# Four buffers for gathered token rows in the experts, and transpositions six steps ahead instead of seven

## The chip, the cores and the metric

The kernel runs on one core of a Trainium2 chip. A core has TensorE (matrix products, writing to PSUM), VectorE, ScalarE and GpSimd (elementwise work), SyncE (which here issues most transfers) and 16 DMA engines between HBM and the on-chip memory SBUF. Each engine works through its own queue in order. The metric is the device time of one execution, in microseconds.

## The reference, cut to what matters

Three networks in a row: attention with a threshold, a mixture of eight experts with one expert for each token, and a dense network with h - tanh(h) in the middle.

```python
# 4 sequences, 8 heads, 576 positions, 64 columns
scores = 1/sqrt(64) * q @ k.T
scores = where(scores >= max(scores) - tau, scores, -1e9)
x = softmax(scores) @ v                      # -> 2304 tokens x 512
logits = x @ w_gate                          # 512 x 8
expert_idx = argmax(logits, axis=1)
gate_w = softmax(logits)[expert_idx]
for e in range(8):
    xe = x[expert_idx == e]
    out[expert_idx == e] = gate_w * (maximum(xe @ w1[e], 0) @ w2[e])   # 512 -> 1024 -> 512
h = out @ w_in                               # 512 -> 2048
return (h - tanh(h)) @ w_out                 # 2048 -> 512
```

## The kernel before, in words

The kernel writes every instruction out by hand, in program order; a small table of numbers (`TB`) sets in which *step* of the expert and dense stages each job stands. The order on each engine is the program order, and the framework adds the waits.

**Attention** fills the first 350 us. Its results go to a table of token rows in HBM (`rows`, 512 columns in FP32), and the gate's logits L gather in SBUF (128 partitions x 8 experts x 18 tokens).

**Routing** (`route`) finds each token's expert and its place there, almost wholly on VectorE: a maximum over the experts, a comparison, a second maximum that breaks ties, the one-hot O, two matmuls for prefix counts, a prefix sum (`rst` restarts it at each expert), and some twenty small operations. It ends with 18 comparisons B (L656; the profile names the line of the helper, L597), which with R (L654, GpSimd) are the operands of 18 matmuls; their result `idx` lists, in columns of 128, the tokens of each expert. Small tiles of the routing live in three places: constants in a pool `c` for the whole program, `keep` and `free` in the expert stage's pool, whose room the attention stage has used before.

**Experts.** The experts are sorted by size, and each has a fixed capacity: 256, 544, 416, 384, 336, 320, 288 and 272 tokens. There are nine *passes* (the second expert has two, of 256 and 288). A pass p begins at step g = 8p and has eight steps. In each step TensorE computes the hidden product of 128 hidden units for the pass's tokens (`h_exp`, L1040, 12 matmuls: the FP32 operands are split in a high and a low half, three products each), then come the step's jobs, then the product with w2 for the step before last (`y_exp`, L1095, 12 matmuls into four PSUM tiles). ScalarE and VectorE make the high and low half of the ReLU (`relu`, L1075 and L1076) at the start of a step. `y` tiles of finished passes are copied by ScalarE (`yo`, L1098) and stored.

The jobs of steps: weight loads (`wload`) and splits (`wsplit`, L1008 on ScalarE and L1010 on VectorE or GpSimd), conversions of the dense network's weights (`conv`, L1155 to L1166), the late part of the routing (`route_late`), and for each chunk m of up to 128 tokens of a pass three jobs: `gather_exp` (L1057, an indirect DMA that GpSimd issues, into a buffer `xr`, in step g - 10 + m), `trans` (L1017, four transpositions by TensorE into the one PSUM tile `t`, in step g - 7 + m), and `evac` (L1027 on ScalarE and L1031 on VectorE, the split into high and low halves `xa`, right behind it). Pass 0 gathers ahead of the steps, transposes in steps -7 and -6, and uses two other PSUM tiles. Between steps -6 and -5, at -5.5, stand `offsets` and `starts` (L673, L680 and small operations of the helpers L570 and L573): 15 VectorE operations that compute where each pass's result goes. Steps below 0 hold jobs alone. The buffers `xr` are three; in the dense stage `x_load` uses them too.

**The dense network** takes the last 450 us, on six blocks of 384 tokens, 16 steps each.

Of the kernel before, what the change touches and what calls it, by code (L numbers as in the profile page):

```python
# [11 lines left out]
F32 = mybir.dt.float32  # L12
F32R = mybir.dt.float32r
F16 = mybir.dt.float16
# [4 lines left out]
ALU = mybir.AluOpType  # L19
# [4 lines left out]
B, H, S, D = 4, 8, 576, 64  # L24
NT, DM = B * S, H * D
# [403 lines left out]
E, F1, F2 = 8, 1024, 2048  # L429
# [6 lines left out]
NTL = 18  # L436
# [30 lines left out]
class Moe:  # L467
# [24 lines left out]
    def consts(self):  # L492
        nc, c, one = self.nc, self.cp.tile, self.attn.one.tile
        z = one([1, DM], F32, name="zrow")
        nc.gpsimd.memset(z, 0.0)
        nc.sync.dma_start(out=self.xtok[ZR:ZR + 1], in_=z)
        self.wg = c([128, 4, E], F32, name="wg")
        nc.sync.dma_start(out=self.wg, in_=self.wgd.rearrange("(k p) e -> p k e", p=128))
        self.i8 = self.iota("i8", E)
        self.r8 = self.iota("r8", E, -1, E)  # L500
        self.j8 = self.iota("j8", E, 1, -1)
        nc.gpsimd.memset(self.j8[:, 0:1], float(E - 1))
        self.i128 = self.iota("i128", 128)
        self.i128h = c([128, 128], F16, name="i128h")
        nc.vector.tensor_copy(self.i128h, self.i128)
        self.ina8 = self.iota("ina8", NMAIN, 128)
        rt = c([128, (E + 2) * NTL], F32, name="rt")
        self.m, self.tm = rt[:, 0:NTL], rt[:, NTL:2 * NTL]
        self.eq = rt[:, 2 * NTL:].rearrange("p (e t) -> p e t", e=E)
        self.ina = self.iota("ina", NMAIN)  # L510
        self.k18 = self.iota("k18", NTL, 128)
        ones = one([128, 128], F32, name="ones")
        nc.gpsimd.memset(ones, 1.0)
        tri = one([128, 128], F32, name="tri")
        nc.gpsimd.affine_select(out=tri, in_=ones, compare_op=ALU.is_gt, fill=0.0, base=0,
                                pattern=[[1, 128]], channel_multiplier=-1)
        self.onesh = c([128, 128], F16, name="onesh")
        self.trih = c([128, 128], F16, name="trih")
        nc.vector.tensor_copy(self.onesh, ones)
        nc.vector.tensor_copy(self.trih, tri)  # L520
        self.O = c([128, E, NTL + 1], F16, name="O")
        nc.gpsimd.memset(self.O, 0.0)

        self.rst = c([128, E, NTL + 1], F32, name="rst")
        nc.gpsimd.memset(self.rst, 1.0)
        nc.gpsimd.memset(self.rst[:, :, 0:1], 0.0)

        self.rc = c([128, 2, E], F32, name="rc")
        for r in range(E):
            b = 128 * CB[r]  # L530
            for i, x in enumerate((b, CAPS[r])):
                nc.gpsimd.memset(self.rc[:, i, r:r + 1], float(x))

        ti = one([128, NTL], I32, name="tok_i")
        for P in range(NP):
            b0, t0 = 2 * P * S + P - ZR, 9 * P
            for i in range(2):
                q = slice(64 * i, 64 * i + 64)
                for o, n, b in ((0, 4, b0 + i), (4, 1, b0 + (S if i else 8)), (5, 4, b0 + S + 1 + i)):
                    nc.gpsimd.iota(ti[q, t0 + o:t0 + o + n], pattern=[[2, n]], base=b, channel_multiplier=9)  # L540
        self.tok = c([128, NTL], F32, name="tok")
        nc.vector.tensor_copy(self.tok, ti)
# [29 lines left out]
    def red(self, o, a, op=ALU.add):  # L572
        self.nc.vector.tensor_reduce(out=o, in_=a, axis=AX.X, op=op)  # L573
# [12 lines left out]
    def route(self, K, T, psum):  # L586


        nc, cp = self.nc, self.cp
# [6 lines left out]
        k_out = lambda x: x.unsqueeze(2).to_broadcast([128, E, E])  # L596
        ts = lambda o, x, s1, s2, op0, op1=None: V.tensor_scalar(out=o, in0=x, scalar1=s1, scalar2=s2, op0=op0, **({"op1": op1} if op1 else {}))  # L597

        m, eq, tm = self.m, self.eq, self.tm
        red(m, te(L), ALU.max)  # L600
        tt(eq, L, bt(m), ALU.is_equal)
        tt(eq, eq, be(self.r8), ALU.mult)
# [16 lines left out]
        loc, lo, h1, ov = K([128, NTL], I32), T([128, NTL]), T([128, NTL]), K([128, NTL])  # L619
# [3 lines left out]
        B, R = T([128, NTL, 128], F16), T([128, NTL, NMAIN], F16)  # L623
# [29 lines left out]
        tt(A, self.ina8.unsqueeze(1).to_broadcast([128, NTL, NMAIN]), h1.unsqueeze(2).to_broadcast([128, NTL, NMAIN]), ALU.is_equal)  # L653
        nc.gpsimd.tensor_tensor(out=R, in0=A, in1=self.tok.unsqueeze(2).to_broadcast([128, NTL, NMAIN]), op=ALU.mult)  # L654
        for t in range(NTL):
            ts(B[:, t], self.i128h, lo[:, t:t + 1], None, ALU.is_equal)  # L656

        self.idx = cp.tile([128, NMAIN], I32, name="idx")
        self.table(B, R, psum("h", [128, NMAIN]), self.idx)
# [239 lines left out]
NW = MB * 128  # L899
# [19 lines left out]
class Mlp(Moe):  # L919
# [57 lines left out]
    def at(self, i, f, *a):  # L977
        self.sched.setdefault(i, []).append((f, a))
# [27 lines left out]
    def wsplit(self, r, i, j):  # L1006
        h, l, raw = self.W.pop((r, i, j, "raw"))
        self.nc.scalar.copy(h, raw)  # L1008
        pool = j if r < E else self.TB["eng"][2 * i + j] == "P"
        (self.nc.gpsimd if pool else self.nc.vector).tensor_tensor(out=l, in0=raw, in1=h.bitcast(F32), op=ALU.subtract)  # L1010
# [41 lines left out]

    def gather_exp(self, p, m, n):
        r, c0, _ = PASS[p]
        t = self.sp.tile([128, DM], F32, tag="xr", name="xr", bufs=3)
        c = CB[r] + c0 // 128 + m
        self.nc.gpsimd.indirect_dma_start(out=t[0:n], out_offset=None, in_=self.xtok, in_offset=bass.IndirectOffsetOnAxis(  # L1057
            ap=self.idx.bitcast(U32)[0:n, c:c + 1], axis=0))
        self.xr["e", p, m] = t
# [114 lines left out]
    def x_load(self, k):  # L1174
        nc = self.nc
        c = slice(NW * k, NW * k + NW)
        self.gb = self.sp.tile([128, DM], F32, tag="xr", name="xr", bufs=3)[:, 0:NW]
        nc.sync.dma_start(out=self.gb, in_=self.gscr.rearrange("(o a) b -> o (a b)", o=1)[:, c].to_broadcast([128, NW]))
        self.xw = []
        for d in range(4):  # L1180
            n, tg, nb = (NW, "yu"[d % 2], 2) if k == 0 else (DM, "xr", 3) if d < 2 else (1024, "raw", 4)
            w = self.sp.tile([128, n], F32, tag=tg, name="xw", bufs=nb)[:, 0:NW]
            nc.sync.dma_start(out=w, in_=self.yT[d][:, c])
            self.xw.append(w)
        t = self.sp.tile([128, max(6 * NMAX, 8 * NW)], F32R, tag="lxb" if k % 2 else "lxa", name="xk")
        t = t[:, 0:8 * NW].rearrange("p (a k n) -> p a k n", a=2, k=4)
        self.xs["l", k] = [(0, t[:, 0], t[:, 1])]
# [70 lines left out]
    def early2(self):  # L1258

        for i, j in FIRST:  # L1260
# [1 line left out]

    TB = {"wl": (4, 5), "ws": (2, 3), "ga": 10, "tr": 7, "ev": 7,
          "last": ((-3, -2), (-1, 1), (-2, 0), (0, 2), (-1, 2), (0, 3), (1, 2), (4, 6), (-60, -55), (-53, -50), (-7,
                  -1), (-6, -4), (5, 10), (9, 11), (11, 12), (12, 14)), "x0": (12, 9, 7), "x": (14, 13, 8),
          "conv": (0, 1, 3, 5, 7, 10, 11, 13, 15, 16, 18, 20, 21, 23, 25, 28, 29, 32, 33, 35, 37, 38, 40, 42, 44, 46,
# [2 lines left out]
    def plan(self, K):  # L1271
        at = self.at
        for p, (r, c0, n) in enumerate(PASS):
            g = 8 * p
            at(g - 8, self.x_exp, p)
            for m in range(-(-n // 128)):
                w = min(128, n - 128 * m)
                if p:
                    at(max(g - self.TB["ga"], -8) + m, self.gather_exp, p, m, w)
                at(g - self.TB["tr"] + m, self.trans, ("e", p, m), w)  # L1280
                at(g - self.TB["ev"] + m, self.evac, ("e", p, m), 128 * m, w)
        B = self.TB
        at(-5.5, self.offsets)
# [75 lines left out]
```

## Time and profile before

| what | value |
|---|---|
| median of 3 runs | 1076.59 us (1075.49 to 1080.34) |
| the profiled execution | 1076.63 us |
| its span, first to last instruction | 1074.5 us |
| granted TensorE clock, mean over the span | 0.944 of 2.4 GHz |
| routing, logits complete to idx | 350.0 to 361.8 us |
| expert stage, first hidden product | 369.95 us |

The profile gives each engine's busy time, what an engine waited for, and the granted clock of TensorE in any stretch. Times within the execution count from the first instruction. A wait that the profile calls "issue" has no releaser that it can name. A row's bracket tells how long the engine was idle before it and what ended that.

### The profile page before, as it was taken

What the parts mean: (1) busy time and instruction counts of PE and PEld (TensorE: products, weight loads), DVE (VectorE), ACT (ScalarE), POOL (GpSimd) and SP (SyncE); (2) the same over time, 40 slices, a digit from 0 to 9 for tenths busy, and PEclk for the clock granted to TensorE, in tenths of its full rate; (3) what the DMA queues carried; (4) which work ended last, traced back from release to release, by engine and by line L of the source; (5) the groups of instructions that cost most, each with busy time, mean ns of one, the idle gap of its engine ahead of it and who ended that gap; (6) DMA issues with size and microseconds to landing.
All of it is one profiled execution on the core that took longest, in us unless ns stands there. A gap on an engine that the chain in (4) does not pass through costs nothing.

```text
span 1074.5 us, 20770 instructions
## 1 busy us (share of the span) xinstructions
PE 957.3 (89%) x7342; PEld 876.6 (82%) x7342; DVE 895.3 (83%) x1635; ACT 671.5 (62%) x1262; POOL 730.7 (68%) x645
## 2 busy tenths in 40 slices
PE   4688897887787488999999988999999999999997
PEld 3576786776677387989999988888999999998986
DVE  5899888888884698977798876998989889888894
ACT  5797887986974154444455557666665666656662
POOL 3897887886874364455656567787867768677763
PEclk9698888898988599999999999999999999999999
DMA  6798999998989485877787976220101101000000
GB/s 160 145 213 165 211 205 152 225 202 163 175 155 169 149 292 199 278 227 247 258 290 252 295 247 177 76 76 20 40 8 38 30 20 40 8 31 1 20 11 30
DMA packets 247368, 153.16 MB, mean 143 GB/s; under 512 B 179642, under 2 KB 222028, under 8 KB 247261
## 3 DMA queue, kind: packets, MB, share of 16 engines
q1 hardware_dynamic: 243501, 141.02, 53.2%
q0 software_dynamic: 3312, 10.49, 2.8%
q8 instruction: 59, 0.97, 0.4%
q14 instruction: 48, 0.39, 0.1%
q10 hardware_dynamic: 448, 0.30, 0.1%
HBM read 85.08 MB, written 23.60 MB: 101 GB/s over the span
## 4 chain that ended last, share of the span: by engine, by line
PE 50%; DVE 9%; issue 3%; DMA 2%; ACT 1%; POOL 0%; another core or an unknown queue 0%; POOLq 0%; DVEq 0%; SPq 0%; ACTq 0%
PE h L1040 25%; PE y L1123 15%; PE y L1095 9%; DVE w L1236 2%; DVE w L1237 2%; PE t L1017 1%; DVE w L1234 1%; DMA xr<-rows,idx 1%; DVE cv L1157 1%; DVE tm L1235 1%; DVE w L1238 1%; DMA raw<-in_moe_w_dram 1%; DVE w L1010 1%; DMA raw<-wscr 0%; DVE cm L1159 0%
## 5 line engine op out<-in xcount | busy, mean ns | idle before, releaser
L265 POOL TENSOR_TENSOR e<-em,e 128x1024 f16<-128x1024 f32 (+1 forms) x98 | 158.1, 1613 | 55.0 <-ACT e L261 23.5
L1233 POOL TENSOR_SCALAR tm<-u 128x384 uint8<-128x384 f32 x88 | 129.7, 1474 | 51.4 <-ACT u L1229 50.8
L1040 PE MATMUL h<-xa,w 128*128 128x256 f32 (+6 forms) x864 | 140.5, 313 | 7.6 <-DVE hbuf L1076 6.8
L1095 PE MATMUL y<-hbuf,w 128*128 128x256 f32 (+6 forms) x864 | 139.5, 310 | 0.6 <-ACT yo L1098 0.6
L1040 PEld LDWEIGHTS h<-xa,w 128*128 128x128 f32 x864 | 130.5, 194 | 9.9 <-DVE hbuf L1076 8.1
L240 ACT ACTIVATE e<-sps,n 128x576 f32<-128x576 f32 x144 | 110.6, 768 | 34.8 <-DVE n L234 33.7
L1010 POOL TENSOR_TENSOR w<-raw,w 128x1024 fp32r<-128x1024 f32 x36 | 91.8, 2551 | 56.0 <-ACT w L1008 28.8
L1095 PEld LDWEIGHTS y<-hbuf,w 128*128 128x128 f32 x864 | 127.5, 191 | 1.3 <-ACT yo L1098 0.8
L1236 DVE SCALAR_TENSOR_TENSOR w<-y,w 128x384 f32<-128x384 f32 x96 | 123.3, 1284 | 0.0
L1229 ACT ACTIVATE u<-h 128x384 f32<-128x384 f32 x96 | 47.1, 491 | 117.3 <-PE h L1040 116.4
L253 DVE SCALAR_TENSOR_TENSOR em<-sps,n,e 128x576 f32<-128x576 f32 x144 | 116.6, 810 | 4.0 <-ACT e L240 2.4
L234 DVE TENSOR_REDUCE n<-sps 128x1 f32<-128x576 f32 x144 | 107.1, 744 | 12.3 <-PE sps L226 11.8
L1250 POOL TENSOR_TENSOR gl<-w,gh 128x384 fp32r<-128x384 f32 x83 | 85.7, 1032 | 38.0 <-ACT gh L1249 38.0
L1040 PE MATMUL h<-xk,w 128*128 128x384 f32 x576 | 109.6, 338 | 0.7 <-DVE w L1010 0.5
L297 PE MATMUL ops<-vh,et 128*128 128x64 f16 (+1 forms) x2240 | 97.4, 201 | 13.0 <-DVE x L303 12.1
L1040 PEld LDWEIGHTS h<-xk,w 128*128 128x128 f32 x576 | 102.1, 188 | 5.6 <-DVE w L1010 1.3
L297 PEld LDWEIGHTS <-et 128*128 128x128 f16 (+1 forms) x2240 | 83.6, 107 | 25.3 <-issue 21.1
L261 ACT CAST e<-em 128x576 f16<-128x576 f32 x144 | 99.9, 695 | 1.2 <-DVE em L253 1.2
L1075 ACT ACTIVATE hbuf<-h 128x256 fp32r<-128x256 f32 (+6 forms) x72 | 31.2, 433 | 108.3 <-PE h L1040 108.2
L226 PE MATMUL sps<-ka,qa 128*128 128x288 f32 x320 | 87.7, 367 | 9.4 <-DVE em L253 5.7
L1008 ACT CAST w<-raw 128x1024 fp32r<-128x1024 f32 x72 | 75.6, 1051 | 21.4 <-DVE free L597 11.6
L1123 PE MATMUL y<-w,gh 128*128 128x512 f32 x258 | 81.1, 395 | 3.2 <-POOL w L1010 1.5
(228 smaller groups left out, 2296.8 us busy)
## 6 DMA issues: line engine op xcount, KB each, us to landing
raw<-in_moe_w_dram SPq DMA_DIRECT2D x64, 512.0 KB, 5.2
cv<-in_moe_w_in_dram SPq DMA_DIRECT2D x16, 512.0 KB, 5.0
cv<-in_moe_w_out_dram SPq DMA_DIRECT2D x16, 512.0 KB, 5.4
wscr<-cm SPq DMA_DIRECT2D x32, 256.0 KB, 3.2
raw<-wscr SPq DMA_DIRECT2D x16, 512.0 KB, 3.8
xw<-yT SPq DMA_DIRECT2D x24, 192.0 KB, 2.7
vv<-in_v_dram SPq DMA_DIRECT2D x8, 512.0 KB, 5.1
raw<-in_q_dram SPq DMA_DIRECT2D x6, 576.0 KB, 7.7
```

Source lines behind the costliest of these rows:

```text
L234: nc.vector.tensor_reduce(out=n[:, 0:1], in_=ps[:, :, 0:288], axis=AX.XY, op=ALU.max, negate=True)
L240: nc.scalar.activation(out=e, in_=ps[:, :, 0:288], func=AF.Exp, bias=n[:, 0:1])
L253: nc.vector.scalar_tensor_tensor(out=self.em[u, g][:, i].rearrange("p (a b) -> p a b", a=2), in0=ps[:, :, 0:288], scalar=n[:, 1:2], in1=e, ...
L261: self.nc.scalar.copy(self.e16[u, g][:, i, 0:S], self.em[u, g][:, i])
L265: eng.tensor_tensor(out=e16[:, r, S + 64:], in0=em[:, r, 0:512], in1=e16[:, r, 0:512], op=ALU.subtract)
L297: nc.tensor.matmul(o[q], lhsT=et[:, base + c, q], rhs=vh[:, a, j, c if c < 5 else c - 5, :], start=(n == 0), stop=(n == len(terms) - 1))
L1010: (self.nc.gpsimd if pool else self.nc.vector).tensor_tensor(out=l, in0=raw, in1=h.bitcast(F32), op=ALU.subtract)
L1040: self.nc.tensor.matmul(out, lhsT=a, rhs=b, start=(i == 0), stop=(i == len(parts) - 1))
L1095: nc.tensor.matmul(self.ys[d], lhsT=a[:, f % 2, s], rhs=b, start=(f == 0 and i == 0), stop=(f == 7 and i == 2))
L1123: nc.tensor.matmul(self.ys[m], lhsT=a[:, s], rhs=b[:, f % 2], start=(f == 0 and i == 0), stop=(f == 15 and i == 2))
L1233: nc.gpsimd.tensor_scalar(out=mk, in0=u, scalar1=RCUT * RCUT, scalar2=None, op0=ALU.is_gt)
L1236: V.scalar_tensor_tensor(out=w, in0=y, scalar=b, in1=w, op0=ALU.add, op1=ALU.mult)
```

## The change

Room is made in SBUF and spent on a fourth buffer `xr`; with it, `trans` and `evac` stand in step g - 6 + m instead of g - 7 + m, while the gathers keep their steps. The room comes from constants: the gate weights move to a pool of the attention stage, the FP16 copy of the row 0..127 goes (B then reads the FP32 row), the tiles for the comparison and the second maximum move to the scratch `free`, and `rst` is FP16.

```diff
-        self.wg = c([128, 4, E], F32, name="wg")
+        self.wg = one([128, 4, E], F32, name="wg")
...
-        self.i128h = c([128, 128], F16, name="i128h")
-        nc.vector.tensor_copy(self.i128h, self.i128)
...
-        rt = c([128, (E + 2) * NTL], F32, name="rt")
-        self.m, self.tm = rt[:, 0:NTL], rt[:, NTL:2 * NTL]
-        self.eq = rt[:, 2 * NTL:].rearrange("p (e t) -> p e t", e=E)
+        self.m = c([128, NTL], F32, name="m")
...
-        self.rst = c([128, E, NTL + 1], F32, name="rst")
+        self.rst = c([128, E, NTL + 1], F16, name="rst")
...
-        m, eq, tm = self.m, self.eq, self.tm
+        m, eq, tm = self.m, T([128, E, NTL]), T([128, NTL])
...
-            ts(B[:, t], self.i128h, lo[:, t:t + 1], None, ALU.is_equal)
+            ts(B[:, t], self.i128, lo[:, t:t + 1], None, ALU.is_equal)
...
-        t = self.sp.tile([128, DM], F32, tag="xr", name="xr", bufs=3)
+        t = self.sp.tile([128, DM], F32, tag="xr", name="xr", bufs=4)
...
-    TB = {"wl": (4, 5), "ws": (2, 3), "ga": 10, "tr": 7, "ev": 7,
+    TB = {"wl": (4, 5), "ws": (2, 3), "ga": 10, "tr": 6, "ev": 6,
```

The same `bufs` stands in `x_load`. The order of instructions on GpSimd and on SyncE is the same in both kernels. On VectorE, at the start of the expert stage, this stood before (`xa` is the split of a chunk; `keep` and `poff` are the operations of `offsets` and `starts`; `hbuf` is the low half of the ReLU):

```order
L1031 TENSOR_TENSOR xa<-y_6252,xa 128x4x128
L1031 TENSOR_TENSOR xa<-y_6260,xa 128x4x128
L570 TENSOR_TENSOR keep<-keep 128x64
L573 TENSOR_REDUCE keep<-keep 128x8
L673 SCALAR_TENSOR_TENSOR keep<-rst,keep 128x8
L570 TENSOR_TENSOR keep<-keep 128x8
L570 TENSOR_TENSOR keep<-keep 128x64
L573 TENSOR_REDUCE keep<-keep 128x8
L680 TENSOR_SCALAR poff<-keep 128x1 x9
L1076 SCALAR_TENSOR_TENSOR hbuf<-h,hbuf 128x256 x2
L1031 TENSOR_TENSOR xa<-t,xa 128x4x128
```

and this stands there now, at the same place of VectorE's queue:

```order
L1027 TENSOR_TENSOR xa<-y_6251,xa 128x4x128
L566 TENSOR_TENSOR keep<-keep 128x64
L569 TENSOR_REDUCE keep<-keep 128x8
L669 SCALAR_TENSOR_TENSOR keep<-rst,keep 128x8
L566 TENSOR_TENSOR keep<-keep 128x8
L566 TENSOR_TENSOR keep<-keep 128x64
L569 TENSOR_REDUCE keep<-keep 128x8
L676 TENSOR_SCALAR poff<-keep 128x1 x9
L1027 TENSOR_TENSOR xa<-y_6273,xa 128x4x128
L1072 SCALAR_TENSOR_TENSOR hbuf<-h,hbuf 128x256 x3
L1027 TENSOR_TENSOR xa<-t,xa 128x4x128
```

The split of pass 0's second chunk has moved behind the 15 operations of `offsets` and `starts`, and the split of pass 1's first chunk behind the ReLU of step 2.

Further on in VectorE's queue, in steps 9 to 11, where pass 2's first two chunks are split (`cv` and `cm` are a conversion, `w` is a weight split), this stood before:

```order
L1159 TENSOR_SCALAR cm<-cv 128x512
L1076 SCALAR_TENSOR_TENSOR hbuf<-h,hbuf 128x256
L1031 TENSOR_TENSOR xa<-t,xa 128x3x128
L1031 TENSOR_TENSOR xa<-t,xa 128x128
L1164 SCALAR_TENSOR_TENSOR cm<-cv,cm 128x512
L1076 SCALAR_TENSOR_TENSOR hbuf<-h,hbuf 128x256
L1031 TENSOR_TENSOR xa<-t,xa 128x3x128
L1031 TENSOR_TENSOR xa<-t,xa 128x128
L1010 TENSOR_TENSOR w_6625<-raw,w_6624 128x1024
```

and this stands there now:

```order
L1155 TENSOR_SCALAR cm<-cv 128x512
L1072 SCALAR_TENSOR_TENSOR hbuf<-h,hbuf 128x256
L1160 SCALAR_TENSOR_TENSOR cm<-cv,cm 128x512
L1072 SCALAR_TENSOR_TENSOR hbuf<-h,hbuf 128x256
L1027 TENSOR_TENSOR xa<-t,xa 128x3x128
L1027 TENSOR_TENSOR xa<-t,xa 128x128
L1006 TENSOR_TENSOR w_6623<-raw,w_6622 128x1024
```

Each chunk's split stands one ReLU half later. On TensorE the four transpositions of a chunk stand one hidden product and one y product later in the same way, from pass 1 on.

## Rows read from the trace of the kernel before

**Rows 1.** The page's engine totals: busy us, share of the span, instructions.

```profile
PE 957.3 (89%) x7342; PEld 876.6 (82%) x7342; DVE 895.3 (83%) x1635; ACT 671.5 (62%) x1262; POOL 730.7 (68%) x645
```

**Rows 2.** Stretches: length, busy PE, PEld, DVE, ACT, POOL (instructions), clock, DMA share, GB/s.

```profile
366.00:400.00 34.00, 30.56 (x220) 28.92 (x220) 25.48 (x42) 14.95 (x24) 19.55 (x12) 0.87 0.78 258
400.00:420.00 20.00, 13.92 (x105) 13.57 (x105) 16.36 (x29) 9.43 (x21) 10.92 (x7) 0.91 0.63 207
...
500.00:540.00 40.00, 40.00 (x239) 39.85 (x238) 32.40 (x42) 19.68 (x36) 22.28 (x14) 1.00 0.80 260
```

**Rows 3.** Waits of TensorE, 366 to 620 us: us in total, times, longest.

```profile
PE h L1040 <- DVE hbuf L1076: 4.6, 3, 2.5
PE t L1017 <- issue: 4.5, 1, 4.5
PE t L1017 <- DMA xr<-rows,idx: 1.6, 1, 1.6
```

**Rows 4.** Timeline, end of attention and routing: start us, us, instruction, idle before.

```profile
348.24 0.62 SPq L316 DMA_DIRECT2D rows<-x  x1
...
350.70 0.31 DVE L570 TENSOR_TENSOR rt<-L,rt 128x144 f32<-128x144 f32 x1
...
352.59 0.47 DVE L626 TENSOR_TENSOR_SCAN keep<-rst,t 128x152 f32<-128x152 f32 x1 [0.46 <-PE t L608]
```

**Rows 5.** The line of that store (L316), 347.5 to 349 us.

```profile
DMA to landing us min/median/max: 2.7/2.7/2.7
```

**Rows 6.** VectorE's B (ns min/median/max), and a copy (us, mean ns).

```profile
L597 DVE TENSOR_SCALAR free<-i128h,free x18: 241/243/962, 357.6 to 361.1; 128x128 f16<-128x128 f16 x18
...
L505 DVE CAST i128h<-i 128x128 f16<-128x128 f32 x1 | 0.2, 227 | 0.0
```

**Rows 7.** Timeline of VectorE and of TensorE's weight loads, start of the experts.

```profile
369.25 1.38 DVE L1031 TENSOR_TENSOR xa<-y,xa 128x512 fp32r<-128x512 f32 x2 [4.72 <-ACT xa L1027]
370.54 0.25 DVE L570 TENSOR_TENSOR keep<-keep 128x64 f32<-128x64 f32 x1
...
371.89 0.63 DVE L680 TENSOR_SCALAR poff<-keep 128x1 int32<-128x1 f32 x9
373.90 0.42 DVE L1076 SCALAR_TENSOR_TENSOR hbuf<-h,hbuf 128x256 fp32r<-128x256 f32 x1 [1.39 <-ACT hbuf L1075]
...
370.68 4.66 PEld L1040 LDWEIGHTS h<-xa,w 128*128 128x128 f32 x23 [0.44 <-DVE xa L1031]
```

**Rows 8.** Timelines of VectorE and of TensorE, 378 to 393 us.

```profile
378.81 0.69 DVE L1031 TENSOR_TENSOR xa<-t,xa 128x512 fp32r<-128x512 f32 x1 [0.47 <-ACT xa L1027]
...
392.11 0.41 DVE L1076 SCALAR_TENSOR_TENSOR hbuf<-h,hbuf 128x256 fp32r<-128x256 f32 x1
...
392.57 1.70 PE L1040 MATMUL h<-xa,w 128*128 128x256 f32 x12 [1.47 <-DVE hbuf L1076]
```

**Rows 9.** Timeline of TensorE, steps 9 to 11.

```profile
401.65 0.63 PE L1017 MATMUL t<-ident,xr 128*128 128x128 f32 x4 [1.62 <-DMA xr<-rows,idx]
...
409.62 1.09 PE L1017 MATMUL t<-ident,xr 128*128 128x128 f32 x4 [4.46 <-issue]
410.36 2.60 PE L1095 MATMUL y<-hbuf,w 128*128 128x256 f32 x12
412.80 1.58 PE L1040 MATMUL h<-xa,w 128*128 128x256 f32 x12
```

**Rows 10.** Timeline of the other engines in the same steps.

```profile
404.19 2.52 DVE L570 TENSOR_TENSOR keep<-keep 128x18 int32<-128x18 f32 x1
404.30 2.37 POOL L1010 TENSOR_TENSOR w<-raw,w 128x1024 fp32r<-128x1024 f32 x1
...
408.72 1.19 ACT L1098 COPY yo<-y 128x256 f32<-128x256 f32 x4
408.77 0.74 DVE L1031 TENSOR_TENSOR xa<-t,xa 128x384 fp32r<-128x384 f32 x2
```

**Rows 11.** A stretch behind the longer wait; columns as in rows 2.

```profile
411.00:412.00 1.00, 1.00 (x7) 1.00 (x7) 0.58 (x2) 1.00 (x3) 0.55 (x1) 0.50 0.36 125
```

More of the change, by code (lines that the diff above doesn't have):

```diff
@@ L1176, in x_load @@
         c = slice(NW * k, NW * k + NW)
-        self.gb = self.sp.tile([128, DM], F32, tag="xr", name="xr", bufs=3)[:, 0:NW]
+        self.gb = self.sp.tile([128, DM], F32, tag="xr", name="xr", bufs=4)[:, 0:NW]
         nc.sync.dma_start(out=self.gb, in_=self.gscr.rearrange("(o a) b -> o (a b)", o=1)[:, c].to_broadcast([128, NW]))
@@ L1180, in x_load @@
         for d in range(4):
-            n, tg, nb = (NW, "yu"[d % 2], 2) if k == 0 else (DM, "xr", 3) if d < 2 else (1024, "raw", 4)
+            n, tg, nb = (NW, "yu"[d % 2], 2) if k == 0 else (DM, "xr", 4) if d < 2 else (1024, "raw", 4)
             w = self.sp.tile([128, n], F32, tag=tg, name="xw", bufs=nb)[:, 0:NW]
```

## The prediction

> **What bounds the kernel now.** I first read the engine totals of the page, to see which engine could set the span: TensorE is busy for 957.3 of 1074.5 us [rows 1], so only about 117 us of the span are open to any change that does not take work off TensorE. Then I read the busy times by stretch from the end of the routing on [rows 2]. The reader should see two different stages there. Between 366 and 400 us TensorE is busy for 30.56 of 34.00 us, between 400 and 420 us for 13.92 of 20.00; between 500 and 540 us it is busy for all 40.00 us. The table of waits for 366 to 620 us says who caused the gaps [rows 3]: the change speaks of two of them, a transposition of gathered rows that waits 1.6 us for its gather and one that waits 4.5 us for something that the profile cannot name ("issue"); 4.6 us more are waits of the hidden product for the ReLU's low half on VectorE. From 500 us on TensorE has no gap to close [rows 2], so the reachable gain lies ahead of that, and it cannot be much more than 1.6 + 4.5 + 4.6 = 10.7 us of waits plus the slow clock behind them.
>
> **Part by part: the routing.** The five first routing operations wrote tiles of their own; now the comparison and the maximum behind it write to the stage's scratch tile, whose room the attention stage used. So the wait for that stage's last stores, which stood at the prefix sum, stands two operations after the logits are complete. Before, the comparison began at 350.70 us and the prefix sum at 352.59 us [rows 4]. The last store is issued at 348.24 us [rows 4] and lands 2.7 us later [rows 5], at 350.94. So the comparison waits 350.94 - 350.70 = 0.24 us, and behind it in VectorE's queue is the whole routing, on which the gathers depend: +0.2 us on the path. Bounds: nothing, if the other engines' waits cover it, and 352.59 - 350.70 = 1.9 us, since the same wait was over by the prefix sum.
>
> The 18 one-hot rows B read a 128-column row of FP16 before and one of FP32 now. One took 243 ns in the median, one 962 ns, beside the GpSimd operation on R [rows 6]. No row shows the FP32 form. The nearest one is a copy of the same 128 columns from FP32 to FP16, 227 ns [rows 6], no slower than the old form; so the lower end is 0. The upper end is the FP32 tensor-tensor operation of 144 columns, 0.31 us [rows 4], 66 ns more, 18 x 66 = 1.2 us. I take 0.3 us, near the copy, all on the path, since the table's last matmul needs the last B. The prefix sum's data0 in FP16, the removed copy of i128 in the attention stage, and the gate weights in another pool I cost at nothing: the sum already mixes types with its PSUM operand, the copy is one of 227 ns [rows 6] in a stage with other work on VectorE, and the load of the gate weights is the same transfer.
> The Trainium skill ("VectorE: DVE Perf Modes", section "The perf-mode tier table") gives a tensor-scalar operation four elements a cycle for 16-bit operands and two for FP32. By that each B costs 32 cycles at 0.96 GHz more, an estimate of 33 ns, so 0.6 us in place of 0.3 and a total of 1078.3 us. The copy in the trace speaks against a large price but does not decide between the two.
>
> **The second chunk of the first pass.** Both chunks were split (L1031) on VectorE in one piece from 369.25 to 370.63 us, and only then came the position operations, from 370.54 us, and the nine starts, until 372.52 us, with VectorE idle for 1.39 us behind them: they were hidden [rows 7]. Now the second chunk's split stands behind all 15 of them. They take 372.52 - 370.54 = 1.98 us. TensorE's second matmul of the first hidden product needs that split: it started at 370.68 us, released by it [rows 7]. So the expert stage starts 2.0 us later. Nothing else covers it, as TensorE has no other ready work there. What could take back a part is the stall at 392.57 us, but that one hangs on VectorE's queue, which moves along. Bounds: 0 (if that queue has slack) and 2.4 us (2.0 and a part of low clock).
>
> **VectorE between 379 and 393 us.** Pass 1's second chunk is also split a step later: its 0.69 us stood at 378.81 us, with slack around it, and now stand in front of the weight conversions, at the head of a run of VectorE work that ends with the ReLU half at 392.11 us, for which TensorE waits 1.47 us [rows 8]. I add 0.7 us; bounds 0 and 1.2 us, since VectorE was idle for 0.47 us in front of it, waiting for ScalarE's half [rows 8], and may be so again.
>
> **Where the gain is: steps 9 to 11.** In step 9 the first transposition for pass 2 waits until 401.65 us; in step 10, behind a hidden product, the second waits until 409.62 us [rows 9]. It writes the one PSUM tile t, which the first chunk's evacuation must have left. VectorE was late with that: an operation of 18 columns that began at 404.19 us took 2.52 us beside GpSimd's weight split of 404.30 us, and ScalarE's four copies of yo began only at 408.72 us [rows 10], behind a conversion in its queue that needs VectorE's part first. With the transpositions a step later TensorE does not meet the gather (landed by 401.65), so the hidden product of step 10 starts at once, 1.6 us earlier, and so does the first transposition. But the y product of step 8, next in line, needs the PSUM tiles that those yo copies release. It gets its first 3 of 12 matmuls done, and then waits until about 409.05 us, a third of a us after 408.72. So the stall of 4.5 us does not go, it changes its name. From there 9 matmuls at the low clock, 2.60 / 12 = 0.22 us each [rows 9], end at 411.0 us, and the next hidden product starts then, where it started at 412.80 us before [rows 9]. Gain: 1.8 us. Bounds: all of 1.6 + 4.5 + 1.5 of low clock (the row of 411 us shows the clock at 0.50, which is 1.2 GHz [rows 11]; the two products took 2.60 and 1.58 us for 12 matmuls, the two transpositions 1.09 and 0.63) = 7.6 us, or a loss of 4.4 us (the third rival).
>
> From 465 us on nothing is waited for that this moves: the trailing transpositions end four steps ahead of their use. GpSimd's and SyncE's orders do not change at all, so the fourth buffer moves no gather; what it does is let a buffer be held a step longer.
>
> **The sum**, on the profiled execution of 1076.63 us: + 0.2 + 0.3 + 2.0 + 0.7 - 1.8 = + 1.4, so 1078.0 us. The median of before is 1076.59 us, the same within 0.1 us, so no correction is due. What a measurement can tell from no change is 0.5%, 5.4 us either way: 1071.2 to 1082.0. The forecast is no measurable change.
>
> **Rivals.**
> *The gather was hidden anyway.* If the yo copies come later than I read them, by the 1.8 us, the whole of the gain is gone and the start remains: 1076.63 + 3.2 = 1079.8 us. For it: the fourth buffer moves no gather. Against: the wait of 1.6 us was a real one for the gather.
> *All stalls break up (faster).* With the split of the first chunk out of step 9, VectorE has 0.74 us less [rows 10] in the step in which the four yo copies stand, and if its operation at 404.19 us misses GpSimd's by this, the 7.6 us go, and with VectorE ahead also the 4.6 us of the hidden product [rows 3]: 1076.63 + 3.2 - 12.2 = 1067.6 us. Against it: GpSimd's order is the same, so it will collide with something on VectorE again.
> *Two stalls for one (slower).* The place is steps 11 and 12: the second and third transpositions of pass 2 each wait for the evacuation of the one tile t, and that now stands behind one ReLU half more on VectorE. If VectorE comes to the first evacuation later than the hidden product of step 11 ends (about 412.5 us), TensorE stops there again, for up to the 4.5 us that it waited for the same tile before, with 1.5 us of low clock behind it. With the 1.6 us of the gather's wait gone that is + 3.2 - 1.6 + 4.5 + 1.5 = + 7.6 and 1084.2 us. For it: VectorE was late with this tile before. Against: it is idle for 20.00 - 16.36 = 3.64 us between 400 and 420 us [rows 2], so it can catch up.
>
> **Chances.** Forecast 0.45, the hidden gather 0.16, all stalls gone 0.18, two stalls 0.21. The first two lie within 0.5%, so 0.61 for no change, 0.18 for faster, 0.21 for slower. The bounds give 1076.63 - 7.6 + 0 = 1069.0 at the low end; at the high end 1.9 + 1.2 + 2.4 + 1.2 + 4.4 = 11.1 would be 1087.7, all at once, which is unlikely, so I stop at 1086. The likeliest case alone spans 1075 to 1081 us.
>
> **What would show it.** The comparison of the routing with a wait for stores of about 0.2 us ahead of it; a B of about 260 ns; the second chunk's split 2 us behind the first's, and TensorE's first steady product waiting for it; no wait of a transposition for a gather; a y product in step 10 that waits for yo. I am wrong if TensorE's start does not move against the gathers' landing, or if the gap between 400 and 413 us closes.

## The result, and the profile after

The changed kernel takes 1086.18 us in the median of 4 runs (1083.51 to 1087.93), against 1076.05 us (1075.49 to 1080.34) for the kernel before on the same chip. The ratio is 1.0086, with a 95% interval of 1.0057 to 1.0116. It is slower by more than 0.5%, where the forecast was no measurable change (1071.2 to 1082.0 us). The profiled execution of the changed kernel is the longest of the four: 1087.93 us with a span of 1085.8, 11.3 us above that of before.

Milestones of the two profiled executions, in us from the first instruction, show the stages in which the 11.3 us arose:

| from | to | before | after | difference |
|---|---|---|---|---|
| start | logits complete (start of the last addition to L) | 350.01 | 354.60 | +4.6 |
| logits | `idx` | 11.59 | 12.60 | +1.0 |
| `idx` | first hidden matmul | 8.35 | 8.18 | -0.2 |
| first hidden matmul | second | 0.73 | 2.75 | +2.0 |
| second hidden matmul | hidden product of step 7 | 21.89 | 21.53 | -0.4 |
| step 7 | hidden product of step 12 | 23.65 | 23.61 | 0.0 |
| step 12 | first product of the dense network | 233.90 | 238.60 | +4.7 |
| dense network | end | 424.4 | 423.9 | -0.5 |

The engine totals of the page (busy us, share of the span, instructions) answer to [rows 1]:

```profile
PE 965.0 (89%) x7342; PEld 884.2 (81%) x7342; DVE 899.5 (83%) x1634; ACT 670.2 (62%) x1262; POOL 727.8 (67%) x645
```

One VectorE instruction is gone (the copy of i128), and TensorE is busy 7.7 us longer with as many matmuls. So part of the loss is not idle time but matmuls at the lower clock.

Busy time by stretch, of the changed kernel, with the columns of [rows 2]:

```profile
500.00:540.00 40.00, 40.00 (x235) 39.83 (x234) 32.11 (x39) 18.86 (x33) 21.60 (x13) 1.00 0.80 255
580.00:620.00 40.00, 36.58 (x240) 36.07 (x240) 31.25 (x42) 19.75 (x38) 19.38 (x12) 0.91 0.76 241
```

The first row is as full as before. The second is new to the argument: between 580 and 620 us TensorE is busy for 36.58 us at a clock of 0.91, where it was busy for 38.86 us at 1.00 in the kernel before:

```profile
580.00:620.00 40.00, 38.86 (x280) 38.20 (x278) 32.38 (x43) 19.90 (x35) 24.41 (x14) 1.00 0.87 282
```

The prediction rests on the row of 500 to 540 us alone and concludes from it that the rest of the stage was closed.

Waits of TensorE in the changed kernel, 366 to 630 us (total, times, longest), answer to [rows 3]:

```profile
...
PE h L1036 <- DVE hbuf L1072: 4.9, 3, 2.5
PE t L1013 <- issue: 2.5, 1, 2.5
PE y L1091 <- ACT yo L1094: 2.4, 1, 2.4
PE h L1036 <- DVE xa L1027: 2.2, 1, 2.2
```

The transposition's wait for a gather (1.6 us) is gone, the "issue" wait of 4.5 us has become one of 2.5 us, and the y product now waits 2.4 us for `yo`, as forecast. But the "issue" wait of 2.5 us ends at 589.6 us and not at 409, and the wait for `xa` is the start of the stage.

### The profile page after: what moved, and what is told of

The parts are those of the page before. It is cut to its first block, busy times and chain, and to the rows that moved or that the text cites. A ratio compares the mean times of both kernels' runs of the same rounds, so it can differ in the third digit from the quotient of the medians.

```text
span 1085.8 us, 20762 instructions
## 1 busy us (share of the span) xinstructions
PE 965.0 (89%) x7342; PEld 884.2 (81%) x7342; DVE 899.5 (83%) x1634; ACT 670.2 (62%) x1262; POOL 727.8 (67%) x645
## 4 chain that ended last, share of the span: by engine, by line
PE 48%; DVE 11%; issue 3%; ACT 2%; DMA 1%; POOL 1%; another core or an unknown queue 0%; POOLq 0%; DVEq 0%; ACTq 0%; SPq 0%
PE h L1036 24%; PE y L1119 15%; PE y L1091 8%; DVE w L1232 2%; DVE w L1233 2%; DVE cv L1153 1%; DVE w L1006 1%; DVE w L1230 1%; PE t L1013 1%; DVE cm L1151 1%; DMA raw<-in_moe_w_dram 1%; DVE tm L1231 1%; DVE w L1234 1%; DMA raw<-wscr 0%; ACT w L1004 0%
## 5 line engine op out<-in xcount | busy, mean ns | idle before, releaser
L1091 PE MATMUL y<-hbuf,w 128*128 128x256 f32 (+6 forms) x864 | 142.4, 315 | 2.4 <-ACT yo L1094 2.4
L1091 PEld LDWEIGHTS y<-hbuf,w 128*128 128x128 f32 x864 | 130.4, 194 | 3.2 <-ACT yo L1094 2.7
L1232 DVE SCALAR_TENSOR_TENSOR w<-y,w 128x384 f32<-128x384 f32 x96 | 121.5, 1265 | 0.0
L1233 DVE SCALAR_TENSOR_TENSOR w<-y,w 128x384 f32<-128x384 f32 x96 | 76.7, 799 | 10.0
```

What stands on the lines that cost most here:

```text
L1091: nc.tensor.matmul(self.ys[d], lhsT=a[:, f % 2, s], rhs=b, start=(f == 0 and i == 0), stop=(f == 7 and i == 2))
L1232: V.scalar_tensor_tensor(out=w, in0=y, scalar=b, in1=w, op0=ALU.add, op1=ALU.mult)
```

## The experiments

Four theories stood against each other. **A**: the steps themselves cost the time (the start, and later in the expert stage transpositions that wait for the one PSUM tile `t`). **B**: the constants made attention and routing slower, which the +4.6 us in the table suggests. **C**: what the start loses is taken back by a later stall. **D**: VectorE is late whatever waits for it, so that without the one tile the wait would only go over to the next product. Ratios are to the kernel before on the same chip, with 95% intervals.

**The steps put back.** The changed kernel with the transpositions again seven steps ahead. The fourth buffer and the constants stay.

```diff
-"tr": 6, "ev": 6
+"tr": 7, "ev": 7
```

> The changed kernel with the transpositions and splits back at seven steps ahead; four buffers and the smaller routing constants stay. Theory A (the later step costs: 2.0 us at the start of the experts, and stalls of TensorE on the one tile t in passes 2 and 7, about 6.5 us with the low clock behind them): 1077 to 1078 us, 1.1 us above before for the routing alone, the first hidden product right behind the second transposition, no wait of a transposition at pass 7. Rival B (the attention stage, 4.6 us later in the profile of after, is slower through the moved tiles or the missing copy): it stays at 1081 to 1082 us, with the logits complete at 354 to 355 us.

Measured: 1081.15 us, ratio 1.0010 [0.9992, 1.0029]. The constants and the buffer alone cost 0.10%, which can't be told from nothing and is 0.29% at most, so most of the loss of 0.59 to 0.86% comes with the steps: **B is refuted** as the main cause. Its profile shows attention ending at 354.02 us, as late as in the changed kernel's first profile, in a kernel of no measurable loss.

**Only the steps.** The kernel before with its three buffers and all its constants, everything one step later.

```diff
-"ga": 10, "tr": 7, "ev": 7
+"ga": 9, "tr": 6, "ev": 6
```

> The kernel before with gathers nine and transpositions six steps ahead: three buffers, all constants as before, only the steps one later. Theory A: 1083 to 1085 us, with the 2.0 us at the start and stalls of transpositions as in the changed kernel. Rival B: the attention as before (350 us), so 1078 to 1080 us at most.

Measured: 1080.27 us, 1.0018 [1.0000, 1.0036]. Less than the changed kernel loses. Its profile shows why. The pass of 320 tokens is 2.6 us longer than before, and there stands the same wait, in a kernel without any of the change's constants:

```profile
584.94 0.40 PE L1017 MATMUL t<-ident,xr 32*128 32x32 f32 x4 [2.70 <-issue]
```

But the first pass takes 58.95 us, against 58.68 before, although its second hidden matmul waits 1.96 us at the start: here the steps that follow pay the start back, which they do not in the changed kernel (60.58 and 60.41 us in its two profiles). The pass of 416 tokens is 1.5 us shorter than before, but this is no merit of the steps. In both kernels its first steps hold the same wait for VectorE, and only the clock behind it differs (the first row is of the kernel before):

```profile
463.42 4.09 PE L1040 MATMUL h<-xa,w 128*128 128x416 f32 x12 [2.53 <-DVE hbuf L1076]
465.54 2.55 PE L1040 MATMUL h<-xa,w 128*128 128x416 f32 x12 [2.58 <-DVE hbuf L1076]
```

In the two profiles of the changed kernel this product takes 2.54 and 3.27 us behind a wait of 2.53 us, so the price varies between executions of one kernel.

**The start repaired.** The changed kernel with the 15 operations of `offsets` and `starts` behind the second chunk's split again.

```diff
-at(-5.5, self.offsets)
-at(-5.5, self.starts)
+at(-4.5, self.offsets)
+at(-4.5, self.starts)
```

> The changed kernel with the position operations and starts in step -4.5, behind the second chunk's split again. Theory A: 2.0 us faster than the changed kernel, 1084 us, the second matmul of the first hidden product 0.7 us behind the first as before. Rival C (the delay at the start is taken back by VectorE's stall ahead of step 7): no difference, 1086 us.

Measured: 1083.76 us, 1.0041 [1.0024, 1.0059]. The profile shows 36 hidden matmuls in one row from the first chunk on, with no wait behind the first of them; the later row is the wait for the tile `t`, which stays.

```profile
373.38 6.67 PE L1036 MATMUL h<-xa,w 128*128 128x256 f32 x36 [0.68 <-ACT xa L1023]
...
587.27 0.40 PE L1013 MATMUL t<-ident,xr 32*128 32x32 f32 x4 [2.45 <-issue]
```

So the repair takes the wait at the start away, but only that: the kernel is still slower than before by 0.24 to 0.59%.

**The buffer used for the gathers.** The changed kernel with the gathers a step earlier and the transpositions seven ahead.

```diff
-"ga": 10, "tr": 6, "ev": 6
+"ga": 11, "tr": 7, "ev": 7
```

> The changed kernel with transpositions seven and gathers eleven steps ahead, so that the fourth buffer lets a gather begin earlier. Theory A: the 1.6 us that a transposition waited for its gather are gone and the tile t's wait stays, 1075 to 1077 us. Rival B: 1080 to 1082 us.

Measured: 1080.03 us, 1.0002 [0.9989, 1.0014]. The fair comparison is the run with the steps put back, which has the same constants (1.0010): an earlier gather buys nothing that can be told from it. The wait for a gather shrinks from 1.6 to 0.7 us, and the "issue" wait behind it stands at 4.0 us instead of 4.5.

**The changed kernel again**, on another chip, beside the next three.

> The changed kernel, word for word, once more, on one chip with the kernels beside it. Theory A (fixed costs: routing 1.0 us, start 2.0 us, expert stage about 4 us more; the rest of the 0.86% was the attention stage of the runs, which varies by some 4 us from run to run in any kernel): ratio 1.005 to 1.007. Rival B (the attention stage is slower by the change): 1.008 to 1.010, with the logits complete at 354 us again.

Measured: 1083.71 us (1083.24 to 1086.07), 1.0059 [1.0044, 1.0074]. The loss repeats at 0.6%. The first result, 0.86%, has an interval that overlaps with this one. In the profile attention ends at 351.05 us, 3.5 us earlier than in the first profile of the same kernel. So **most of the +4.6 us of attention is variation between executions.** Over the twelve profiles, with the same attention work in each, that time is between 347.5 and 354.6 us (350.0, 352.1, 347.5 and 349.4 with the constants of before; 354.6, 354.0, 352.2, 350.3, 351.05, 351.1, 350.3 and 348.45 with changed ones). The means of the two groups are 349.8 and 351.5 us, so a remainder of up to 2 us from the change cannot be excluded.

**A second PSUM tile for the transpositions.** The changed kernel; every second chunk's transposition writes to a PSUM tile of the y products instead of `t`.

```diff
-ps = self.psum("t" if key[1] else f"y{4 - key[2]}", ...)
+ps = self.psum(("t" if key[2] % 2 == 0 else f"y{4 * key[1] % 5}")
+               if key[1] else f"y{4 - key[2]}", ...)
```

> The changed kernel with one thing else: the odd chunks' transpositions of passes 1 to 8 go to the PSUM tile of the pass's own first y product, which is free until that pass's y product begins, so that a transposition does not need the evacuation of the chunk in front of it. Theory A (the one tile t makes TensorE wait for VectorE): the waits of transpositions that the profile calls issue (2.5 us in pass 7) go, and with them the low clock behind; 3 to 5 us faster than the changed kernel. Rival D (VectorE is late whatever waits for it): the wait goes over to the next hidden or y product, and the time stays within 1 us.

Measured: 1080.88 us, 1.0030 [1.0014, 1.0047], so 0.29% less than the changed kernel on the same chip (1.0059). Its waits of TensorE from 480 to 630 us, and the timelines of TensorE and VectorE where the changed kernel waits:

```profile
PE h L1036 <- DVE hbuf L1072: 2.3, 1, 2.3
...
```

```profile
585.97 0.43 PE L1013 MATMUL t<-ident,xr 32*128 32x32 f32 x4
586.33 2.02 PE L1091 MATMUL y<-hbuf,w 128*128 128x320 f32 x12
588.19 1.92 PE L1036 MATMUL h<-xa,w 128*128 128x320 f32 x12
...
584.86 2.50 DVE L1155 TENSOR_SCALAR cm<-cv 128x512 f32<-128x512 f32 x1
587.28 0.48 DVE L1072 SCALAR_TENSOR_TENSOR hbuf<-h,hbuf 128x320 fp32r<-128x320 f32 x1
587.68 0.74 DVE L1027 TENSOR_TENSOR xa<-y,xa 128x384 fp32r<-128x384 f32 x2
```

VectorE is as late as in the changed kernel (its 2.50 us operation, then the ReLU half, then the split at 587.68), but the transposition at 585.97 no longer waits for that split, and the two products behind it run in 2.02 and 1.92 us. **A holds here and D is refuted at this place**: the wait comes from the one tile `t`, and no other wait of its size takes it over.

**The start's cost alone.** The kernel before with the 15 operations in front of the second chunk's split.

```diff
-at(-5.5, self.offsets)
-at(-5.5, self.starts)
+at(-6.5, self.offsets)
+at(-6.5, self.starts)
```

> The kernel before with the position operations and starts in step -6.5, so that pass 0's second split stands behind them, as in the changed kernel; nothing else. Theory A: 2.0 us slower than before, ratio 1.0015 to 1.0025, the second hidden matmul 2.7 us behind the first. Rival C: taken back ahead of step 7, ratio 1.000.

Measured: 1080.83 us, 1.0023 [1.0008, 1.0038], or 2.5 us [0.9, 4.1].

```profile
367.41 0.58 PE L1040 MATMUL h<-xa,w 128*128 128x256 f32 x1 [0.68 <-ACT xa L1027]
370.13 5.28 PE L1040 MATMUL h<-xa,w 128*128 128x256 f32 x23 [2.14 <-DVE xa L1031]
```

The cost of the wait of 2.14 us reaches the end of the kernel. **C is refuted** for the start by itself: no later stall takes it back.

**All repairs together.** The changed kernel with six steps, the operations of the start at -4.5, two tiles, and the row 0..127 and the tiles `eq` and `tm` in FP16 as constants.

```diff
-self.i128 = self.iota("i128", 128)
+self.i128 = self.iota("i128", 128, dt=F16)
+self.eq, self.tm = c([128, E, NTL], F16, name="eq"), c([128, NTL], F16, name="tm")
...
-m, eq, tm = self.m, T([128, E, NTL]), T([128, NTL])
+m, eq, tm = self.m, self.eq, self.tm
```

> The changed kernel with the costs taken away one by one: operations of step -5.5 behind the second split, two PSUM tiles for transpositions, the row 0..127 kept in FP16 alone (B as before, and 256 bytes freed), the comparison's tiles in FP16 outside the scratch, so that nothing in front of the prefix sum waits for the attention's stores. Theory A: routing as before (11.6 us from logits to idx), start as before, no transposition waits for VectorE: 0 to 4 us faster than before, ratio 0.996 to 1.000. Rival D: VectorE's lateness shows at other waits, ratio 1.002 to 1.004.

Measured: 1075.96 us, 0.9977 [0.9963, 0.9990]: faster than the kernel before by 0.23%, and than the changed one by 0.8%. Its routing takes 11.51 us (before 11.59), its first hidden matmul to the dense network 279.79 us (before 280.17). Its waits of TensorE, 366 to 630 us:

```profile
PE h L1037 <- DVE hbuf L1073: 8.0, 4, 2.6
PE y L1014 <- DMA xr<-rows,idx: 5.6, 1, 5.6
PE y L1092 <- ACT yo L1095: 3.3, 1, 3.3
PE h L1037 <- DVE w L1007: 2.2, 2, 1.6
```

No transposition waits for anything any more (the first wait for a gather, of pass 0, stays in all kernels). The waits that remain are the hidden product's for VectorE's ReLU half and weight split, and the y product's for `yo`. This one profile is 0.9 us shorter than before's, less than the 2.5 us of the ratio, and which stage gives the rest is open.

**The second tile alone**, in the kernel before (the same edit as above).

> The kernel before, three buffers, seven steps, all constants as they were, with the second PSUM tile for odd chunks' transpositions alone. If the gain of the kernel best over before comes from the second tile alone (the wait of 4.5 us in step 10), it is as fast as best: ratio 0.997 to 0.999. If it needs the later step and the fourth buffer too (the y product behind the transposition waits for yo in any case), the wait only goes over to that product: ratio 0.999 to 1.001.

Measured: 1078.25 us, 1.0000 [0.9982, 1.0018]. Its waits, 366 to 630 us, and the transposition of step 10:

```profile
PE y L1017 <- ACT yo L1098: 5.3, 2, 4.9
...
409.43 1.12 PE L1017 MATMUL y<-ident,xr 128*128 128x128 f32 x4 [4.87 <-ACT yo L1098]
```

The "issue" wait of 4.5 us of [rows 3] is gone, and in its place the transposition itself (L1017) waits 4.9 us. The second tile is one of the `y` tiles, and this one still holds a result of pass 0 until ScalarE copies it to `yo`. So the stall changed its name to the one that the prediction gave, `yo`, though not on the y product. The run doesn't tell what a tile that is free at this place would be worth; that the y product behind it, which needs the same copies, would then wait in its turn is likely but not shown here.

**All repairs with seven steps** and the gathers at 11. The operations of the start stay at -5.5, which lies behind the split there.

```diff
-"ga": 10, "tr": 6, "ev": 6
+"ga": 11, "tr": 7, "ev": 7
```

> Four buffers used for earlier gathers: gathers eleven and transpositions seven steps ahead, the second PSUM tile, FP16 row and comparison tiles as in best. If six steps ahead has no merit of its own, the same as best: ratio 0.996 to 0.999. If the later step is worth something once nothing waits for tile t, it is slower than best by 1 to 3 us: ratio 0.999 to 1.001.

Measured: 1078.09 us, 0.9990 [0.9975, 1.0005]. Its interval overlaps with that of the version with six steps (0.9963 to 0.9990), so whether six steps themselves have any merit is not settled. Seven steps don't have the tile free in step 10 either: a transposition waits 4.75 us for `yo` there, where the version with six steps waits 3.33 us, on its y product.

## Why the prediction was right or wrong, point by point

**The comparison's wait** was forecast at 0.2 us. The routing of the changed kernel, on SyncE's queue and VectorE, against [rows 4]:

```profile
352.53 0.61 SPq L316 DMA_DIRECT2D rows<-x  x1
...
354.86 0.40 DVE L569 TENSOR_REDUCE m<-L 128x18 f32<-128x144 f32 x1
355.69 0.31 DVE L566 TENSOR_TENSOR free<-L,m 128x144 f32<-128x144 f32 x1 [0.44 <-DVE m L569]
```

The comparison starts 0.44 us behind the maximum, against none before. The bracket names VectorE's own maximum, which had just ended; that the stores are the cause is told by the runs in which the wait is longer. Where VectorE waits 0.64 us (the start repaired), 0.87 us (the second tile) and 1.12 us (the earlier gathers), the bracket reads "DMA rows<-x". The prediction took the landing of the last store as the end of the wait. In this profile the store lands at 352.53 + 2.7 = 355.23 us and the comparison starts 0.46 us behind that; with the second tile it is 0.45 us (352.17 and 352.62). So the place and the cause were right, and the price, 0.4 to 1.1 us, was low by about that step. The prefix sum with `rst` in FP16 takes 0.47 us, as before, so the term put at nothing was right, though not for its reason: the row of before [rows 4] has no mixed types.

**B** was forecast at 0.3 us. The row of the changed kernel (ns min/median/max, first and last start), against [rows 6]:

```profile
L593 DVE TENSOR_SCALAR free<-i,free x18: 275/276/1062, 362.5 to 366.6; 128x128 f16<-128x128 f32 x18
```

276 against 243 ns, and 4.39 against 3.73 us for the 18: +0.66 us. The copy, at 227 ns, that I took for the nearest row did not tell what the comparison costs. The estimate from the Trainium skill ("VectorE: DVE Perf Modes", section "The perf-mode tier table") was 33 ns each and 0.6 us, and the trace agrees with it to the nanosecond. Both terms together account for the routing's +1.0 us, where 0.5 was forecast.

**The start** was forecast at 2.0 us, and comes out so:

```profile
374.85 0.69 DVE L1027 TENSOR_TENSOR xa<-y,xa 128x512 fp32r<-128x512 f32 x1 [4.72 <-ACT xa L1023]
375.46 0.26 DVE L566 TENSOR_TENSOR keep<-keep 128x64 f32<-128x64 f32 x1
...
376.85 0.63 DVE L676 TENSOR_SCALAR poff<-keep 128x1 int32<-128x1 f32 x9
377.39 0.68 DVE L1027 TENSOR_TENSOR xa<-y,xa 128x512 fp32r<-128x512 f32 x1
```

```profile
375.38 0.58 PE L1036 MATMUL h<-xa,w 128*128 128x256 f32 x1 [0.68 <-ACT xa L1023]
378.13 2.29 PE L1036 MATMUL h<-xa,w 128*128 128x256 f32 x9 [2.17 <-DVE xa L1027]
```

The second chunk's split starts 2.54 us behind the first's. Of [rows 7] both halves hold: the 15 operations were hidden before, and now stand between the two splits. TensorE does one matmul and waits 2.17 us.

**VectorE at 379 to 393 us** was forecast at +0.7 us. The wait for the ReLU half of [rows 8] did grow, from 1.47 to 2.00 us, but from the second hidden matmul to the product behind that wait the changed kernel takes 0.4 us less. The term was zero or slightly below.

**Steps 9 to 11** were forecast at -1.8 us. The timelines of the changed kernel there, against [rows 9, 10]:

```profile
410.65 1.68 PE L1036 MATMUL h<-xa,w 128*128 128x256 f32 x10 [1.62 <-DVE w L1006]
412.13 1.05 PE L1013 MATMUL t<-ident,xr 128*128 128x128 f32 x4
412.84 0.99 PE L1091 MATMUL y<-hbuf,w 128*128 128x256 f32 x3
416.24 2.29 PE L1091 MATMUL y<-hbuf,w 128*128 128x256 f32 x9 [2.42 <-ACT yo L1094]
418.33 2.76 PE L1036 MATMUL h<-xa,w 128*128 128x256 f32 x12
420.89 1.05 PE L1013 MATMUL t<-ident,xr 128*128 128x128 f32 x4
...
411.29 2.53 DVE L566 TENSOR_TENSOR keep<-keep 128x18 int32<-128x18 f32 x1
411.40 2.37 POOL L1006 TENSOR_TENSOR w<-raw,w 128x1024 fp32r<-128x1024 f32 x1
...
415.83 1.17 ACT L1094 COPY yo<-y 128x256 f32<-128x256 f32 x4
```

The wait for `yo` is the one forecast, down to the 3 of 12 matmuls before it and the 9 behind it. One step before it was not: the hidden product of step 10 does start without the gather's wait, at 408.56 us, but after two matmuls it waits 1.62 us for the low half of a weight split on VectorE, as long as the gather's wait was. So it ends no earlier against step 7 than before; the gain comes from the transposition and three matmuls that now stand ahead of the wait for `yo`, whose copies begin 16.2 us behind step 7's product in both kernels. VectorE's 18-column operation meets GpSimd's split as before. From step 7's hidden product to step 11's the changed kernel takes 18.67 us against 20.23: a gain of 1.6 us. What I did not count is the step behind: the hidden product of step 11 takes 2.76 us, where it took 1.58 [rows 9], since it comes closer behind the wait and so runs in the low clock (0.50 from 418 to 421.5 us), and the second transposition (1.05 us for its four matmuls), which stood ahead of step 11 before, now stands behind that product. One step later the gain is 0.0 us.

**The step that failed** is the sentence "From 465 us on nothing is waited for that this moves: the trailing transpositions end four steps ahead of their use." The hidden product that uses a transposition does have four steps. The next transposition, which uses the same tile, has one. So a wait was put at nothing that measures 2.3 to 2.7 us, with up to 2.7 us of lower clock behind it. The changed kernel in the pass of 320 tokens, in whose steps the 288 tokens of the next pass are transposed in three chunks (GpSimd, VectorE, then TensorE):

```profile
585.42 2.77 POOL L1006 TENSOR_TENSOR w<-raw,w 128x1024 fp32r<-128x1024 f32 x1
...
585.99 2.49 DVE L1155 TENSOR_SCALAR cm<-cv 128x512 f32<-128x512 f32 x1
588.39 0.48 DVE L1072 SCALAR_TENSOR_TENSOR hbuf<-h,hbuf 128x320 fp32r<-128x320 f32 x1
588.79 0.74 DVE L1027 TENSOR_TENSOR xa<-t,xa 128x384 fp32r<-128x384 f32 x2
...
589.64 0.60 PE L1013 MATMUL t<-ident,xr 32*128 32x32 f32 x4 [2.46 <-issue]
590.17 3.57 PE L1091 MATMUL y<-hbuf,w 128*128 128x320 f32 x12
593.54 3.05 PE L1036 MATMUL h<-xa,w 128*128 128x320 f32 x12
```

and the kernel before at the same work (TensorE, then VectorE):

```profile
578.09 0.43 PE L1017 MATMUL t<-ident,xr 32*128 32x32 f32 x4
578.45 2.02 PE L1095 MATMUL y<-hbuf,w 128*128 128x320 f32 x12
...
576.33 0.74 DVE L1031 TENSOR_TENSOR xa<-t,xa 128x384 fp32r<-128x384 f32 x2
...
580.92 2.53 DVE L1159 TENSOR_SCALAR cm<-cv 128x512 f32<-128x512 f32 x1
```

The reader should follow the order on VectorE. Before, the second chunk's split (576.33) was done 4 us before the operation of 2.5 us beside GpSimd's split (580.92). With the split a step later, it stands right behind that operation and behind the ReLU half, at 588.79, and TensorE, which has finished its hidden product, waits 2.46 us for tile `t`. Behind the wait, the clock (columns as above):

```profile
592.00:594.00 2.00, 2.00 (x9) 2.00 (x9) 0.81 (x1) 0.00 (x0) 0.00 (x0) 0.50 0.77 216
```

0.50 is 1.2 GHz, and the two products there take 3.57 and 3.05 us instead of 2.02 and 1.92. Wait and clock give 2.46 + 1.55 + 1.13 = 5.1 us, and the pass is 35.08 us long against 29.92, 5.2 more. That alone is as much as the table's +4.7 us between step 12 and the dense network; the rest there, up and down, is mostly the clock behind waits that both kernels have. The size differs from run to run by what the clock does behind the wait. The pass takes 33.64 us in the second profile of the changed kernel (wait 2.32, y product 3.51, hidden product 2.01), and 32.24 and 32.49 us with the start repaired and with only the steps, where the wait is 2.45 and 2.70 us and the y product keeps 2.02. All four profiles with six steps and one tile have it; in the eight others the pass takes 29.7 to 30.0 us.

This is the mechanism of the third rival ("Two stalls for one"): a transposition waits for the evacuation of the one tile `t`, which stands one ReLU half later on VectorE, with low clock behind. The rival placed it at steps 11 and 12. There the transposition at 420.89 did not wait; it came true five passes later, where I had excluded it on the strength of a stretch (500 to 540 us) that ends before. So the mechanism was on the list, and the search for its places stopped at the first. The signs that the prediction named nearly all came (the wait for stores, the slower B, the split 2.5 us behind the first, no wait for a gather, the y product that waits for `yo`), and the time was off all the same: none of them looks at the place that failed.

**The sum, by times.** Start alone +0.23%, constants +0.10% (not distinguishable from nothing), tile `t` 1.0059 - 1.0030 = +0.29%: together 0.62%, against 0.59% measured on the second chip. The agreement is closer than the intervals (0.15% or more either way for each), and another pair of runs does not give it: only the steps, 0.18%, and the constants, 0.10%, make 0.28%. In the one profile of the kernel with only the steps the start was paid back within the first pass, so the costs don't simply add up, and why the steps cost more together with the constants stays open. Of the forecast's terms the start was there and, in the changed kernel, not given back; the gain that was to pay for it was not; and the loss at tile `t`, about 3 us in time, was missing. The remaining 0.27% of the first measurement is within the intervals of the two.

The first median, 1086.18 us, lies at the upper end of the range of 1069 to 1086 us. That is luck: the range's upper end adds bounds for other places and doesn't have the wait at 589.6 us in it. At the lower end the range leaves out the prediction's own second rival (1067.6 us).

## What to carry to other kernels

When jobs move by a step, every wait in which they take part moves with them: go through all places of the pattern and not only the first, and for each shared tile ask how far behind its use the *next user of the tile* comes, not only the user of its contents. An operation set in front of a critical one in an in-order queue costs its whole length if nothing later is known to wait longer; moved by itself, it was not given back here. Test a move and its side costs separately: the change lost 0.6 to 0.9%, and the same move with a second PSUM tile, the order of the start mended and FP16 kept for the constants won 0.23%, of which the move's own share is not settled.

## What the runs showed of the hardware

An 18-column VectorE operation takes 2.5 us when it meets GpSimd's weight split: it starts at 411.29 us and ends at 413.82, 0.05 us behind the split's end (411.40 + 2.37 = 413.77), while the operation of the same tile size behind it takes 0.18 us at 413.86. The 512-column operation of 585.99 us ends 0.29 us behind GpSimd's split (588.48 and 588.19) and takes 2.49 us, where the same line takes 0.43 us at 575.58 in the kernel before. So in these rows the price does not hang on VectorE's operation but on how much of GpSimd's is left. The Trainium skill ("SBUF — State Buffer", section "SBUF: two separate sides") describes a port pair that the two engines share, which the one that starts first holds for its whole instruction while the other waits. The ends in this trace agree with the waiting; the order does not show in the starts, since the record of the 18-column operation starts 0.11 us before that of GpSimd's (411.29 and 411.40), and yet VectorE is the one that waits.

The end of attention varies over 7 us (0.7% of the span) between the twelve profiles, and by 3.5 us between two profiles of the same kernel. A difference of one stage between two single profiles is weak evidence below that.

Behind a wait of 2.53 us the clock fell in one profile and not in another of the same kernel: twelve matmuls of 416 columns took 2.54 and 3.27 us in the two profiles of the changed kernel, and 4.09 us in the kernel before, where the granted clock is 0.50 from 465 to 467 us.
